# The last 52 rows of two Z blocks side by side in one buffer, contracted as two 64-row matmuls

## The chip, the cores and the metric

The kernel runs on one core of a Trainium2 chip. The core has a matrix engine (PE), a vector engine (DVE, VectorE), a scalar engine (ACT, ScalarE), GpSimd (POOL) and SP, which issues most of the transfers. Matmuls contract over the 128 partitions of on-chip memory (SBUF) and write to PSUM, eight banks of 512 fp32 values per partition. The metric is the device time of one execution in microseconds (us); 371.29 us is the median of the runs before.

## The reference

Two layers over x of 8 batches, 5696 positions and 128 channels: a long causal convolution by FFT, and a spectral mixing of its first 64 modes with a residual and a ReLU.

```python
L = 2 * S                                   # S = 5696
y = irfft(rfft(x, n=L, axis=1) * rfft(h, n=L, axis=0)[None], n=L, axis=1)[:, :S]

X = rfft(y, axis=1)
Y = zeros_like(X)
Xr, Xi = real(X[:, :64]), imag(X[:, :64])
Y[:, :64] = (einsum('bmd,mde->bme', Xr, w_r) - einsum('bmd,mde->bme', Xi, w_i)) + \
      1j * (einsum('bmd,mde->bme', Xr, w_i) + einsum('bmd,mde->bme', Xi, w_r))
u = y + irfft(Y, n=S, axis=1)
return u + maximum(u @ w_ch, 0)
```

## The kernel before, in words

The position is split as q*64 + p, with 89 values of q and J = 64 of p. The transforms are products with constant matrices, in fp16 with fp32 sums. The batches go in four groups of two (NP = 4).

In the first stage, for each group, PE transforms along q (`a_tile`, matmuls with F and Xin), then along p for each of 90 frequencies k (`second`, matmuls of 64 rows with As and M: batch 0 on partitions 0-63, batch 1 on 64-127, each to its own PSUM bank), the filter is multiplied in (`products`), a further product with W1 and W2 goes back along p (tile Zs or Zt), and the result is stored to a scratch array zs in HBM: 90 x 2 = 180 rows (real and imaginary part of each k) by 64 p by 256 values. Meanwhile `modes` sums up the 64 modes of the output spectrum (XT).

In the mode mixing, PE multiplies XT by the mode weights W, the result Y is transposed with an identity and becomes C, the coefficients of the second layer's inverse transform.

The last stage, the synthesis, makes u and the output. It reads zs back in blocks of ZB = 16 values of p: four blocks per group, 16 in all. A block has 180 rows: the first 128 go to a buffer ZTna (1024 KB), the other 52 to partitions 32 to 83 of a buffer ZTnb (416 KB), whose partitions 0 to 31 GpSimd has cleared once (`clear_zt`). There are NC = 5 such pairs of buffers. `u_tile(i, b, half)` makes eight values of p of block i for batch b, in two PSUM banks: for each bank one product of C with IBs (356 columns) and, for each of four values of p, one product of 89 columns with S4a (128 rows) and one with S4b (84 rows, 32 of them zeros). The tile is then read out to UT by ScalarE or VectorE (`n_ev` decides: VectorE takes counts 1, 4 and 6 of every 8; in the last group ScalarE takes all). The constants S4a and S4b are loaded by half and mirrored to the other half, S4a by VectorE and S4b by ScalarE (`reflect`).

`o_tile` multiplies four columns of 128 positions of UT by WI (w_ch beside an identity, 256 columns each); ScalarE writes the ReLU to R, VectorE adds and writes O, and SP stores to `out_dram`. Output tiles of one group stand between the synthesis tiles of the next; group 0 has none beside it. Both kinds of tile take PSUM banks in turn from four slots of two banks (`LSLOT`).

What sets the order: each engine runs its list in the order in which the program adds to it, and the recorder puts the waits in. SP's list holds the stores to zs, the constants, the block reads and the output stores, so a read waits for all that was added to SP before it. The dictionary `early` names the tick of the last group of stage one at which a read is added: S4b at 8, block 0 at 10, S4a at 12, identity and IBs at 14, block 1 at 16, block 3 at 19 and block 2 at 21; block 4 follows after the loop. From then on block i + 5 is added to SP's list when block i's tiles are done. Three tiles' S4 products are made ahead of need, among the mixing's products (`u_z(..., True)`, `ahead`); the first of them stands ahead of the mixing in PE's list.

All matmuls of this program are recorded at one line, 323, and all DMAs at line 320, so the tiles' names tell them apart.

Of the kernel before, what the change touches and what calls it, by code (L numbers as in the profile page):

```python
# [4 lines left out]
P = 128  # L5
# [118 lines left out]
def bass_long_conv_fft__then__afno_spectral_mix_kernel(nc, x, h, moe_w_r, moe_w_i, moe_w_ch, out):  # L124
# [40 lines left out]
    sg = np.ones((P, 3))  # L165
    sr = np.stack([(-1.0) ** kk, -(-1.0) ** kk], axis=1).reshape(2 * NK)
    sg[:, 0] = sr[0:P]
    sg[PB:PB + RB, 1] = sr[P:2 * NK]
    sg[M:P, 2] = -1.0
    tt = np.arange(S)  # L170
# [79 lines left out]
    wc_sb = at("Wc", 2 * P, F16, take(2 * P * 2))  # L250
    sg_sb = at("SG", 3, F32, take(12))
# [4 lines left out]
    ZB = 16  # L256
# [4 lines left out]
    zt_off = [(a_h, a_h2), (a_as1, a_as1 + 2 * ZP), (a_as1 + 4 * ZP, a_as1 + 6 * ZP), (a_h + 2 * ZP, a_h2 + 2 * ZP),  # L261
              (a_m2, a_g)]
    assert 2 * S + 8 * ZP <= AW * 2
    zt = [[at(f"ZT{i}{'ab'[p_]}", ZP, F16, zt_off[i][p_]) for p_ in range(2)] for i in range(NC)]
    ib_sb = at("IBs", S, F16, a_m)
    s4_sb = [at("S4a", S, F16, a_m + 2 * S), at("S4b", S, F16, a_as)]
    assert 4 * S + 2 * ZP + 4 * P + 2048 <= 2 * MW
# [31 lines left out]
    def bank(i):  # L299
        return ("bank", i)  # L300
# [226 lines left out]
    ZX = [("zs", i, b) for i in range(NZ, NZL) for b in range(2)]  # L527
    zt_old = [(H_ALL, H_ALL), (AST, AST), (AST, AST), (H_ALL, H_ALL), (M_ALL[3:6], G_ALL)]

    def load_zt(i):  # L530
        g_, c_ = divmod(i, J // ZB)
        for part, (p0, r0, n) in enumerate(((0, 0, P), (PB, P, RB))):
            old = list(once(("zt", i % NC, part), zt_old[i % NC][part]))
            dma("sync", bass.AP(zt[i % NC][part], p0 * ZP, [[ZP, n], [1, ZP]]),
                bass.AP(zs, (g_ * 2 * NK + r0) * J * 256 + c_ * ZB * 256, [[J * 256, n], [1, ZP]]),
                "t", [("zd", g_, s_) for s_ in range(NT)], [("zt", i % NC, part)], after=old)

    def clear_zt(i):
        z32 = zt[i][1][0:PB, :].bitcast(U32)
        R.add("gpsimd", lambda e: e.memset(z32, 0), (), [("zt0", i)], after=list(zt_old[i][1]) + pace)  # L540

    def load_ib():
# [11 lines left out]
    def load_s4(part):  # L554
        n = PB + RB if part else P
        dma("sync", s4_sb[part][0:n, 0:SH], bass.AP(c_s4, part * SH, [[2 * SH, n], [1, SH]]), "p", (),
            [("s4", part, 0)], after=AST if part else M_ALL[1:4])
# [13 lines left out]
    pace = []  # L571

# [176 lines left out]
    for g_ in range(NP):  # L749
        if g_ == NP - 1:  # L750
            load_w(0)
            load_w(1)
        for t in range(NT + LM):
            tick(g_, t)
            assert g_ + 1 < NP or not wp
            if g_ == NP - 1 and t in early:
                pace[:] = [("u", min(t, NT - 1) % NU)]
                early[t]()
        evac(bass.AP(xt, 2 * g_ + B, [[B * XTW, P], [B, 2], [3 * B, M], [1, 2]]), pv(MB, 0, [[M, 2], [1, M], [P, 2]]),
             [bank(MB)], [("xt", g_)], 1.0 / 64, eng="scalar", after=[("ag", k) for k in range(NS + 2 * XN, NK)])  # L760
        evac(bass.AP(xt, 2 * g_, [[B * XTW, P], [3 * B, M], [1, 2]]), pv(MB, M, [[1, M], [P, 2]]),
             [bank(MB)], [("xtn", g_)], -1.0 / 64, eng="vector" if g_ + 1 == NP else "scalar", after=[("ag", k) for k in range(NS + 2 * XN, NK)])
        if g_ + 1 < NP:
            for j in range(NB_, 32):
                a_tile(j, [(0, 4, 2, 6)[(j - 5) % 4]], "both" if j == 31 else (A, V)[(j - NB_) % 9 % 2])
                if j == 31:
                    second(g_ + 1, 0, 0, DA)
                if wp and j % 2 == 1:
                    dst, src_, ring, tok = wp.pop(0)
                    dma("gpsimd", dst, src_, ring, (), [tok], after=[("as", j)])  # L770


    pace[:] = []
    load_wi()
    for i in range(4, NC):
        load_zt(i)
        clear_zt(i)

# [4 lines left out]

    def u_z(i, b, half, alone=False, parts=(0, 1)):
        g_, c_ = divmod(i, NCH)
        t = ahead.get((i, b, half))
        if t is None:
            t = turns("l", LSLOT)
        z = zt[i % NC]
        for hb in parts:  # L790
            if not alone:
                u_c(i, b, half, t, hb, True)
            for pl in range(4):
                for ri in range(2):
                    pz = half * 8 + hb * 4 + pl
                    so = (c_ * ZB + pz) * NQ
                    n = (P, PB + RB)[ri]
                    mm(pv(t + hb, pl * NQ, [[1, NQ]]), z[ri][0:n, pz * 256 + b * P:pz * 256 + b * P + P], s4_sb[ri][0:n, so:so + NQ],
                       alone and pl == 0 and ri == 0, not alone and pl == 3 and ri == 1, [("zt", i % NC, ri), ("zt0", i % NC), ("s4", ri, 0)] + ([("s4", ri, 1)] if c_ >= NCH // 2 else []), [bank(t + hb)])
        if alone:  # L800
            ahead[(i, b, half)] = t
        return t

    def u_c(i, b, half, t, hb, first_):
        g_, c_ = divmod(i, NCH)
        pl0 = half * 8 + hb * 4
        mm(pv(t + hb, 0, [[1, 4 * NQ]]), c_sb[:, (2 * g_ + b) * P:(2 * g_ + b + 1) * P],
           ib_sb[:, (c_ * ZB + pl0) * NQ:(c_ * ZB + pl0 + 4) * NQ], first_, not first_,
           [("c", g_ // 2), ("ib", 0)] + ([("ib", 1)] if c_ >= NCH // 2 else []), [bank(t + hb)])

    def u_tile(i, b, half):
        g_, c_ = divmod(i, NCH)
        t = ahead.get((i, b, half))
        if t is None:
            t = u_z(i, b, half)
        else:
            for hb in range(2):
                u_c(i, b, half, t, hb, False)
# [5 lines left out]
        evac(bass.AP(u_sb[ub], c_ * ZB + half * 8, [[S, P], [J, NQ], [4, 2], [1, 4]]),  # L824
             src, [bank(t), bank(t + 1)], [("u_", ub, 2 * c_ + half)], eng=e, after=once(("u", ub), old))
# [32 lines left out]
    reflect("vector", ib_sb, P, 2, ("ib",), M_ALL[0:2])  # L858

# [52 lines left out]
    todo = []  # L912
    NB = NCH * NP
    NW4 = NW // 4
    for g_ in range(NP):
        last = g_ == NP - 1
        order = [(c_, b) for b in range(2) for c_ in range(NCH)] if last else [(c_, b) for c_ in range(NCH) for b in range(2)]
        for n, (c_, b) in enumerate(order):
            i = NCH * g_ + c_
            for half in range(2):  # L920
                u_tile(i, b, half)
                for _ in range((2, 2 + half)[n >= NCH] if last else 1 + half):
# [4 lines left out]
            if last and n == NCH - 1:  # L927
                todo += [(g_, 0, r4) for r4 in range(NW4)]
# [37 lines left out]
```

## Time and profile before

| | |
|---|---|
| median of 3 runs | 371.29 us (371.05 to 375.09) |
| profiled execution, first to last instruction | 370.1 us |
| PE busy, share of the span | 354.7 us, 96% |
| ACT busy | 316.2 us, 85% |
| DVE busy | 291.8 us, 79% |
| POOL busy | 75.2 us, 20% |
| DMA | 103.94 MB, mean 281 GB/s |

The profile gives of its own execution the span alone; the median lies 1.2 us above it. L323 is line 323 of the kernel. A row such as `ps<-S4b,ZT3b 84*128 84x89` is a matmul that writes PSUM from S4b and ZT3b, with 84 rows contracted, 128 columns of weights and 89 moving columns. `PEld` is the load of weights, which overlaps the matmuls. `SPq` is SP issuing a DMA: its duration is that of the issue, and the time to landing is told apart. In the timeline a row has its start, its duration (for merged rows, of all together), and in brackets the idle time of the engine before it with what ended it. Matmuls overlap: the step from one start to the next is what a matmul takes of PE.

### The profile page before, as it was taken

The numbers are of one execution on the slowest core, as the hardware profiler recorded it, in microseconds if no ns is written. First come the engines' busy times: TensorE is split into PE (matmuls) and PEld (weight loads), VectorE is DVE, ScalarE is ACT, GpSimd is POOL, SyncE is SP. The second block draws the span as 40 slices with busy tenths as digits, with TensorE's granted clock in tenths as the row PEclk, the third lists the DMA queues.
The fourth block names the chain that finished last, engine by engine and source line by source line (L and its number), as shares of the span: only waits on it lengthen the run. The fifth ranks groups of instructions, "written<-read, shape, count | busy, mean of one in ns | idle before, by whom it ended". The sixth has DMA issues, their size and how long they took to land.

```text
span 370.1 us, 12455 instructions
## 1 busy us (share of the span) xinstructions
PE 354.7 (96%) x5350; PEld 276.5 (75%) x5350; DVE 291.8 (79%) x332; ACT 316.2 (85%) x499; POOL 75.2 (20%) x117
## 2 busy tenths in 40 slices
PE   7999899999999999999999999999999999999994
PEld 7878766667866668866668766668899888888873
DVE  3549899988999999989999988775357777756666
ACT  8559999999999999999999999995467777688885
POOL 8804012100833311823213001151000000000000
PEclk9999999999999999999999999999999999999999
DMA  7999979969999996999996999999999999999878
GB/s 139 209 271 382 249 165 292 232 198 283 93 140 213 263 258 186 132 160 215 263 278 128 171 310 363 342 345 388 381 410 386 413 410 408 418 399 376 326 291 349
DMA packets 87048, 103.94 MB, mean 281 GB/s; under 512 B 22730, under 2 KB 72522, under 8 KB 83438
## 3 DMA queue, kind: packets, MB, share of 16 engines
q1 hardware_dynamic: 64610, 81.33, 62.5%
q0 software_dynamic: 22384, 21.83, 35.4%
q8 instruction: 42, 0.69, 0.7%
q14 instruction: 12, 0.10, 0.1%
HBM read 70.61 MB, written 51.12 MB: 329 GB/s over the span
## 4 chain that ended last, share of the span: by engine, by line
PE 78%; ACT 10%; DMA 7%; DVE 3%; issue 1%; POOL 1%; DVEq 0%; POOLq 0%
PE ps L323 78%; ACT As L313 6%; DMA out_dram<-O 5%; DMA Hin<-in_h_dram 2%; ACT R L898 1%; DVE As L317 1%; ACT Xs L311 1%; DVE U L623 1%; POOL Hin L320 1%; ACT UT L311 1%; DVE O L899 0%; ACT Zs L311 0%; DVE Hp L438 0%; ACT C L313 0%; DVE Hs L315 0%
## 5 line engine op out<-in xcount | busy, mean ns | idle before, releaser
L652 DVE TENSOR_TENSOR U<-Xs,Hs 128x2048 f16<-128x2048 f16 (+1 forms) x72 | 85.8, 1197 | 12.1 <-ACT Xs L311 11.5
L323 PE MATMUL ps<-U,Wc 128*128 128x512 f16 (+1 forms) x368 | 93.8, 376 | 1.4 <-DVE U L623 1.4
L311 ACT CAST Xs<-ps 128x1024 f16<-128x1024 f32 (+1 forms) x76 | 75.0, 995 | 5.8 <-PE ps L323 3.1
L311 ACT CAST Zs<-ps 128x512 f16<-128x512 f32 (+1 forms) x132 | 70.1, 605 | 0.7
L899 DVE TENSOR_TENSOR O<-ps,R 128x512 f32<-128x512 f32 x81 | 52.4, 684 | 21.6 <-ACT R L898 11.4
L898 ACT ACTIVATE R<-ps 128x512 f32<-128x512 f32 (+1 forms) x92 | 50.5, 592 | 8.5 <-PE ps L323 8.4
L317 DVE TENSOR_SCALAR As<-ps 128x720 f16<-128x720 f32 x64 | 53.1, 879 | 4.8 <-PE ps L323 3.3
L323 PE MATMUL ps<-As,M 64*128 64x128 f16 (+3 forms) x1504 | 52.5, 214 | 2.4 <-ACT As L313 1.2
L313 ACT ACTIVATE As<-ps 128x720 f16<-128x720 f32 (+1 forms) x68 | 48.2, 771 | 5.0 <-PE ps L323 4.8
L323 PE MATMUL ps<-F,Xin 128*128 128x180 f16 x512 | 52.1, 249 | 0.1
L323 PE MATMUL ps<-WI,UT 128*128 128x256 f16 x360 | 50.8, 278 | 0.5 <-ACT UT L311 0.4
L311 ACT CAST UT<-ps 128x712 f16<-128x712 f32 x46 | 34.5, 752 | 19.4 <-PE ps L323 18.4
L323 PEld LDWEIGHTS ps<-U,Wc 128*128 128x128 f16 x368 | 29.1, 97 | 28.2 <-DVE U L623 1.9
L323 PEld LDWEIGHTS ps<-F,Xin 128*128 128x128 f16 x512 | 45.2, 155 | 6.7 <-DVE Xin L365 0.9
L323 PEld LDWEIGHTS ps<-As,M 64*128 64x128 f16 x1504 | 42.2, 94 | 8.7 <-ACT Xs L311 1.9
L323 PEld LDWEIGHTS ps<-WI,UT 128*128 128x128 f16 x360 | 38.9, 152 | 3.2 <-issue 1.8
L323 PE MATMUL ps<-IBs,C 128*128 128x356 f16 x128 | 39.2, 314 | 0.8 <-DVE O L899 0.7
L320 POOL DMA_DIRECT2D Xt<-in_x_dram x40 | 21.4, 540 | 76.5 <-PE ps L323 76.0
L323 PEld LDWEIGHTS ps<-G,Zs 128*128 128x128 f16 x512 | 26.1, 96 | 14.1 <-ACT Zs L311 0.2
L652 DVE TENSOR_TENSOR U<-ps,Hs 128x2048 f16<-128x2048 f32 (+1 forms) x16 | 35.5, 2216 | 0.0
L323 PE MATMUL ps<-G,Zs 128*128 128x128 f16 (+2 forms) x512 | 31.9, 192 | 0.1
L311 ACT CAST Zt<-ps 128x512 f16<-128x512 f32 x52 | 29.1, 659 | 0.0
(76 smaller groups left out, 479.4 us busy)
## 6 DMA issues: line engine op xcount, KB each, us to landing
out_dram<-O SPq DMA_DIRECT2D x39, 512.0 KB, 10.5
zscr<-Zs SPq DMA_DIRECT2D x62, 256.0 KB, 6.7
zscr<-Zt SPq DMA_DIRECT2D x26, 256.0 KB, 6.6
Xt<-in_x_dram POOLq DMA_DIRECT2D x20, 320.0 KB, 6.9
W<-wscr SPq DMA_DIRECT2D x4, 1024.0 KB, 8.5
ZT0a<-zscr SPq DMA_DIRECT2D x4, 1024.0 KB, 11.0
M<-cM POOLq DMA_DIRECT2D x5, 720.0 KB, 17.6
ZT1a<-zscr SPq DMA_DIRECT2D x3, 1024.0 KB, 11.1
```

The costliest lines, as they stand in the source:

```text
L311: R.add(e, lambda h_: h_.copy(dst, src), reads, writes, after=after)
L313: R.add(e, lambda h_: h_.activation(dst, src, COPY, scale=scale), reads, writes, after=after)
L317: R.add(e, lambda h_: h_.tensor_scalar_mul(dst, src, scale), reads, writes, after=after)
L320: R.add(eng, lambda h_: h_.dma_start(dst, src), reads, writes, ring=ring, after=after)
L323: R.add("tensor", lambda h_: h_.matmul(o, l, r, start=st, stop=sp), reads, writes)
L623: R.add("vector", lambda e: e.tensor_tensor(bass.AP(u_s[0], b * 512 + d0, [[2048, P], [1024, 2], [D, n], [1, d1 - d0]]), bass.AP(s_[0], s_ ...
L652: R.add("vector", lambda e: e.tensor_tensor(uv, src, hv, MULT), bk + [("h", t, 0), ("h", t, 1, 0), ("h", t, 1, J)], [("u", i)])
L898: R.add("scalar", lambda e: e.activation(rv, src_r, RELU), bk, [("r", i % NR)], after=once(("r", i % NR), G_ALL + XTT + [("y", 0), ("y", 1 ...
L899: R.add("vector", lambda e: e.tensor_tensor(ov, src_u, rv, ADD), bk + [("r", i % NR)], [key + (h_,)], after=once(key, old))
```

## The change

Two blocks become a pair k (blocks 2k and 2k+1). The first 128 rows of each block keep a buffer of their own (`za`, seven of them). The other 52 rows of both blocks go into one buffer (`zb_`, three of them): those of block 2k to partitions 0-51, those of block 2k+1 to 64-115. Nothing is cleared any more. S4b holds the 52 rows twice likewise, each half with the columns of its own blocks; it is loaded whole (128 x 2848 values) and no longer mirrored.

A tile `u_tile(k, b, h4)` now takes four values of p from each block of the pair, one block per PSUM bank. Its order on PE is both products with IBs, eight with S4a (bank 0, then bank 1), then eight with S4b, of 52 rows, alternating between partitions 0-51 (bank 0) and 64-115 (bank 1). The number of matmuls is the same. The two reads of a pair's 52 rows are issued by SP for the first three pairs, and by ScalarE for pairs 3 to 7, when a pair's tiles are done; the next two `za` reads follow on SP.

```diff
-    RB, PB = 2 * NK - P, 32
+    RB, PB = 2 * NK - P, 64
...
-    s4t = np.zeros((P, 2 * SH))
-    s4t[:, 0:SH] = rows[0:P, 0:SH]
-    s4t[PB:PB + RB, SH:2 * SH] = rows[P:2 * NK, 0:SH]
+    s4b = np.zeros((P, S // 2))
+    for p0 in range(2):
+        s4b[p0 * PB:p0 * PB + RB] = rows[P:].reshape(RB, J // ZB // 2, 2, ZB * NQ)[:, :, p0].reshape(RB, S // 2)
+    s4t = np.concatenate([rows[0:P, 0:SH], s4b], axis=1)
...
-    NC = 5
+    NCA, NCB = 7, 3
...
+    def load_za(i):
         g_, c_ = divmod(i, J // ZB)
+        r_ = i % NCA
+        dma("sync", za[r_][:, :], bass.AP(zs, g_ * 2 * NK * J * 256 + c_ * ZP, [[J * 256, P], [1, ZP]]),
+            "t", zdone(g_), [("za", r_)], after=once(("za", r_), za_old[r_]))
+
+    def load_zb(k):
+        r_ = k % NCB
+        for p0 in range(2):
+            g_, c_ = divmod(2 * k + p0, J // ZB)
+            n = RB - RS
+            dma("scalar" if k >= NCB else "sync", bass.AP(zb_[r_], p0 * PB * ZP, [[ZP, n], [1, ZP]]),
+                bass.AP(zs, (g_ * 2 * NK + P) * J * 256 + c_ * ZP, [[J * 256, n], [1, ZP]]),
+                "t", zdone(g_), [("zb", r_, p0)], after=once(("zb", r_, p0), zb_old[r_]))
...
-             9: lambda: clear_zt(0),
-             10: lambda: load_zt(0),
+             10: lambda: (load_za(0), load_zb(0)),
              12: lambda: load_s4(0),
-             14: lambda: (load_id(), load_ib(), clear_zt(1)),
-             16: lambda: load_zt(1),
-             19: lambda: (load_zt(3), clear_zt(3)),
-             NT - 2: lambda: (load_zt(2), clear_zt(2))}
+             14: lambda: (load_id(), load_ib()),
+             16: lambda: load_za(1),
+             19: lambda: (load_za(2), load_zb(1)),
+             NT - 2: lambda: load_za(3)}
...
-    for i in range(4, NC):
-        load_zt(i)
-        clear_zt(i)
+    load_za(4)
+    load_zb(2)
+    load_za(5)
+    load_za(6)
...
+        for hb in range(2 if 0 in parts else 0):
+            z, r_ = za[(2 * k + hb) % NCA], (2 * k + hb) % NCA
             for pl in range(4):
+                pz = h4 * 4 + pl
+                so = ((c_ + hb) * ZB + pz) * NQ
+                mm(pv(t + hb, pl * NQ, [[1, NQ]]), z[:, pz * 256 + b * P:pz * 256 + b * P + P], s4_sb[0][:, so:so + NQ],
+                   alone and pl == 0, False, [("za", r_)] + ns, [bank(t + hb)])
+        r_ = k % NCB
+        for pl in range(4 if 1 in parts else 0):
+            pz = h4 * 4 + pl
+            so = (c_ // 2 * ZB + pz) * NQ
+            for hb in range(2):
+                r0 = hb * PB
+                mm(pv(t + hb, pl * NQ, [[1, NQ]]), zb_[r_][r0:r0 + RB, pz * 256 + b * P:pz * 256 + b * P + P],
+                   s4_sb[1][r0:r0 + RB, so:so + NQ], False, not alone and pl == 3,
+                   [("zb", r_, hb), ("s4", 1, 0)], [bank(t + hb)])
...
-    reflect("scalar", s4_sb[1], PB + RB, 1, ("s4", 1), AST)
...
-            if b == 1 and i + NC < NB:
-                load_zt(i + NC)
+            if b == 1:
+                if k + NCB < NPR * NP:
+                    load_zb(k + NCB)
+                for i in (2 * k, 2 * k + 1):
+                    if i + NCA < NCH * NP:
+                        load_za(i + NCA)
```

More of the change, by code (lines that the diff above doesn't have):

```diff
@@ L250, in bass_long_conv_fft__then__afno_spectral_mix_kernel @@
     wc_sb = at("Wc", 2 * P, F16, take(2 * P * 2))
-    sg_sb = at("SG", 3, F32, take(12))
+    sg_sb = at("SG", 2, F32, take(8))
     XTW = 3 * M
@@ L260, in bass_long_conv_fft__then__afno_spectral_mix_kernel @@
     a_as1, a_m2 = a_as + 2 * S, a_m + 4 * S
-    zt_off = [(a_h, a_h2), (a_as1, a_as1 + 2 * ZP), (a_as1 + 4 * ZP, a_as1 + 6 * ZP), (a_h + 2 * ZP, a_h2 + 2 * ZP),
-              (a_m2, a_g)]
+    za_off = [a_h, a_as1, a_h + 2 * ZP, a_as1 + 4 * ZP, a_as1 + 6 * ZP, a_m2, a_g]
+    zb_off = [a_h2, a_h2 + 2 * ZP, a_as1 + 2 * ZP]
     assert 2 * S + 8 * ZP <= AW * 2
-    zt = [[at(f"ZT{i}{'ab'[p_]}", ZP, F16, zt_off[i][p_]) for p_ in range(2)] for i in range(NC)]
+    za = [at(f"ZA{i}", ZP, F16, za_off[i]) for i in range(NCA)]
+    zb_ = [at(f"ZB{i}", ZP, F16, zb_off[i]) for i in range(NCB)]
     ib_sb = at("IBs", S, F16, a_m)
-    s4_sb = [at("S4a", S, F16, a_m + 2 * S), at("S4b", S, F16, a_as)]
+    s4_sb = [at("S4a", S, F16, a_m + 2 * S), at("S4b", S // 2, F16, a_as)]
     assert 4 * S + 2 * ZP + 4 * P + 2048 <= 2 * MW
@@ L527, in bass_long_conv_fft__then__afno_spectral_mix_kernel, with zdone @@
     ZX = [("zs", i, b) for i in range(NZ, NZL) for b in range(2)]
-    zt_old = [(H_ALL, H_ALL), (AST, AST), (AST, AST), (H_ALL, H_ALL), (M_ALL[3:6], G_ALL)]
-    def load_zt(i):
-        g_, c_ = divmod(i, J // ZB)
[L532 to L540, printed above, removed]
+    za_old = [H_ALL, AST, H_ALL, AST, AST, M_ALL[3:6], G_ALL]
+    zb_old = [H_ALL, H_ALL, AST]
+    def zdone(g_):
+        return [("zd", g_, s_) for s_ in range(NT)]
+    def load_za(i):
+        g_, c_ = divmod(i, J // ZB)
+        r_ = i % NCA
[9 more added lines that the diff above has]
+                "t", zdone(g_), [("zb", r_, p0)], after=once(("zb", r_, p0), zb_old[r_]))
     def load_ib():
@@ L782, in bass_long_conv_fft__then__afno_spectral_mix_kernel, with u_z @@
     ahead = {}
-    def u_z(i, b, half, alone=False, parts=(0, 1)):
-        g_, c_ = divmod(i, NCH)
-        t = ahead.get((i, b, half))
+    def u_z(k, b, h4, alone=False, parts=(0, 1)):
+        g_, c_ = divmod(2 * k, NCH)
+        t = ahead.get((k, b, h4))
         if t is None:
             t = turns("l", LSLOT)
[L789 to L792, printed above, removed]
-            for pl in range(4):
[L794 to L799, printed above, removed]
+        if not alone:
+            for hb in range(2):
+                u_c(k, b, h4, t, hb, True)
+        ns = [("s4", 0, 0)] + [("s4", 0, 1)] * (c_ >= NCH // 2)
+        for hb in range(2 if 0 in parts else 0):
+            z, r_ = za[(2 * k + hb) % NCA], (2 * k + hb) % NCA
+            for pl in range(4):
+                pz = h4 * 4 + pl
[6 more added lines that the diff above has]
+            so = (c_ // 2 * ZB + pz) * NQ
+            for hb in range(2):
+                r0 = hb * PB
+                mm(pv(t + hb, pl * NQ, [[1, NQ]]), zb_[r_][r0:r0 + RB, pz * 256 + b * P:pz * 256 + b * P + P],
+                   s4_sb[1][r0:r0 + RB, so:so + NQ], False, not alone and pl == 3,
+                   [("zb", r_, hb), ("s4", 1, 0)], [bank(t + hb)])
@@ L800, in u_z, with u_c @@
         if alone:
-            ahead[(i, b, half)] = t
+            ahead[(k, b, h4)] = t
         return t
-    def u_c(i, b, half, t, hb, first_):
-        g_, c_ = divmod(i, NCH)
-        pl0 = half * 8 + hb * 4
+    def u_c(k, b, h4, t, hb, first_):
+        g_, c_ = divmod(2 * k, NCH)
         mm(pv(t + hb, 0, [[1, 4 * NQ]]), c_sb[:, (2 * g_ + b) * P:(2 * g_ + b + 1) * P],
-           ib_sb[:, (c_ * ZB + pl0) * NQ:(c_ * ZB + pl0 + 4) * NQ], first_, not first_,
+           ib_sb[:, ((c_ + hb) * ZB + h4 * 4) * NQ:((c_ + hb) * ZB + h4 * 4 + 4) * NQ], first_, not first_,
@@ L823, in u_tile @@
         src = pv(t, 0, [[1, NQ], [512, 2], [NQ, 4]])
-        evac(bass.AP(u_sb[ub], c_ * ZB + half * 8, [[S, P], [J, NQ], [4, 2], [1, 4]]),
-             src, [bank(t), bank(t + 1)], [("u_", ub, 2 * c_ + half)], eng=e, after=once(("u", ub), old))
+        evac(bass.AP(u_sb[ub], c_ * ZB + h4 * 4, [[S, P], [J, NQ], [ZB, 2], [1, 4]]),
+             src, [bank(t), bank(t + 1)], [("u_", ub, 2 * c_ + h4)], eng=e, after=once(("u", ub), old))
     XTT = [(n, g_) for g_ in range(NP) for n in ("xt", "xtn")]
     reflect("vector", s4_sb[0], P, 0, ("s4", 0), M_ALL[1:4])
-    reflect("scalar", s4_sb[1], PB + RB, 1, ("s4", 1), AST)
     MC = 4
@@ L916, in bass_long_conv_fft__then__afno_spectral_mix_kernel @@
         last = g_ == NP - 1
-        order = [(c_, b) for b in range(2) for c_ in range(NCH)] if last else [(c_, b) for c_ in range(NCH) for b in range(2)]
+        order = [(c_, b) for b in range(2) for c_ in range(NPR)] if last else [(c_, b) for c_ in range(NPR) for b in range(2)]
         for n, (c_, b) in enumerate(order):
[L919 to L922, printed above, removed]
+            k = NPR * g_ + c_
+            for h4 in range(4):
+                u_tile(k, b, h4)
+                for _ in range((2, 2 + h4 % 2)[n >= NPR] if last else 1 + h4 % 2):
                     if todo:
                         o_tile(*todo.pop(0))
-            if b == 1 and i + NC < NB:
-                load_zt(i + NC)
-            if last and n == NCH - 1:
+            if b == 1:
[4 more added lines that the diff above has]
+                        load_za(i + NCA)
+            if last and n == NPR - 1:
                 todo += [(g_, 0, r4) for r4 in range(NW4)]
```

29 lines of the change are left out of this document (13 added, 16 removed).

## The prediction

> **What bounds the kernel now.** I read the page's busy line first, then busy time by stage, then single matmuls, then the transfers with their landing times. The last two of these windows are the synthesis that the change rewrites (it goes on to 357); 247.00:256.40 is the mode mixing before it, with the first products of that synthesis already in it.
>
> ```profile
> span 370.1 us, 12455 instructions
> PE 354.7 (96%) x5350; PEld 276.5 (75%) x5350; DVE 291.8 (79%) x332; ACT 316.2 (85%) x499; POOL 75.2 (20%) x117
> 247.00:256.40 9.40, 8.54 (x210) 7.71 (x208) 3.67 (x6) 5.80 (x8) 4.03 (x4) 1.00 1.07 373
> 256.40:270.40 14.00, 13.96 (x241) 11.99 (x242) 6.18 (x8) 6.67 (x9) 0.00 (x0) 1.00 1.01 390
> 270.40:317.00 46.60, 46.60 (x669) 41.99 (x666) 33.10 (x50) 33.92 (x58) 0.00 (x0) 1.00 1.01 405
> ```
>
> After the length of a stretch come PE, PEld, DVE, ACT and POOL, then the granted clock, the DMA share and GB/s. From 256.4 on PE has no hole, ACT works three quarters of the time at most until 317, and **the 16 DMA engines are full as well** (1.01). So two things set the end of this stage: what PE spends on a tile, and whether a block's read has landed when PE comes to it. How near the second is shows in the waits of PE's weight loads, in two rows of the timeline and in one piece of the chain that ended last:
>
> ```profile
> PEld ps L323 <- DMA ZT2b<-zscr: 0.3, 1, 0.3
> 336.13 0.21 PE L323 MATMUL ps<-S4b,ZT0b 84*128 84x89 f16 x1 [0.16 <-DMA ZT0b<-zscr]
> 338.32 0.31 PE L323 MATMUL ps<-IBs,C 128*128 128x356 f16 x1 [0.33 <-DVE O L899]
> 320.68 16.68 DMA out_dram<-O
> ```
>
> PE already waits for a read twice, and once for DVE, which was held by an output store that took 16.68 us to land and free its buffer. The idle time in brackets counts from the end of the matmul before, and in a stream the next one starts some 0.16 before that end (duration 0.20, step 0.04, rows below); so the steps lost are about 0.3, 0.3 and 0.5 us.
>
> **What a tile costs.** One synthesis tile is, per PSUM bank, one product with IBs and eight of 89 columns. Rows of one bank, then a place where 64-row matmuls (As,M) stand between 128-row ones, and one with 64 columns:
>
> ```profile
> 300.10 0.31 PE L323 MATMUL ps<-IBs,C 128*128 128x356 f16 x1
> 300.25 0.20 PE L323 MATMUL ps<-S4a,ZT3a 128*128 128x89 f16 x1
> 300.29 0.21 PE L323 MATMUL ps<-S4b,ZT3b 84*128 84x89 f16 x1
> 300.59 0.32 PE L323 MATMUL ps<-IBs,C 128*128 128x356 f16 x1
> 301.08 0.30 PE L323 MATMUL ps<-WI,UT 128*128 128x256 f16 x1
> 130.05 0.27 PE L323 MATMUL ps<-G,Zs 128*128 128x128 f16 x2
> 130.10 0.22 PE L323 MATMUL ps<-G,Zs 128*128 128x128 f16 x1
> 130.25 1.07 PE L323 MATMUL ps<-As,M 64*128 64x128 f16 x32
> 131.10 0.22 PE L323 MATMUL ps<-As,M 64*128 64x128 f16 x2
> 131.25 0.39 PE L323 MATMUL ps<-U,Wc 128*128 128x512 f16 x1
> 31.95 0.41 PE L323 MATMUL ps<-Ah,M 64*128 64x64 f16 x16
> 32.29 0.30 PE L323 MATMUL ps<-F,Xin 128*128 128x180 f16 x1
> ```
>
> Look at start times, not durations. Eight 89-column products take 0.34 us (300.25 to 300.59), 0.0425 each, and a tile 0.98 us (300.10 to 301.08). The 32 As products are 16 pairs, one on partitions 0-63 and one on 64-127, each to its own bank: 15 steps from 130.25 to 131.10 are 0.057 per **pair**, what one 128-column product takes alone (130.05 to 130.10). So pairs do run side by side. But the step from the last G product to the first As is 0.15 instead of 0.055, and out again 131.10 to 131.25 is 0.15: **a change between 128 and 64 rows costs PE 0.095 us, each way.** For 64 columns, 0.34 less one such exit leaves 0.031 a pair; a line between 64 and 128 columns gives 0.041 for a pair of 89.
>
> **The change, part by part.**
>
> *Side-by-side products.* A tile's eight S4b products (0.34) become four pairs (4 x 0.041 = 0.164) and two changes of rows (0.19): 0.354, so +0.014; if a pair steps like today's single product, 0.0425, +0.02; with 0.01 more for the first pair, +0.03. Order matters here: the new code puts all S4a products first, so it is two changes per tile, not sixteen. I take +0.02: 64 tiles make +1.3 us, the 48 of pairs 2 to 7 +1.0 (0.7 to 1.4). **What is halved is given back by the switching.** [...]
>
> *What must have landed when.* The reads and their landings:
>
> ```profile
> S4b<-cS SPq DMA_DIRECT2D x1, 481.9 KB
> 241.31 0.56 SPq L320 DMA_DIRECT2D ZT1a<-zscr  x1
> ZT1a<-zscr SPq DMA_DIRECT2D x1, 1024.0 KB, 7.7
> 257.67 2.29 SPq L320 DMA_DIRECT2D ZT4a<-zscr  x1
> ZT4a<-zscr SPq DMA_DIRECT2D x1, 1024.0 KB, 10.2
> 261.25 1.31 SPq L320 DMA_DIRECT2D ZT0a<-zscr  x1
> ZT0a<-zscr SPq DMA_DIRECT2D x1, 1024.0 KB, 10.3
> ZT4b<-zscr SPq DMA_DIRECT2D x1, 416.0 KB
> 248.85 0.20 PE L323 MATMUL ps<-S4a,ZT0a 128*128 128x89 f16 x1
> 249.94 0.25 PE L323 MATMUL ps<-XT,W 128*128 128x64 f16 x3 [0.21 <-issue]
> 270.46 0.20 PE L323 MATMUL ps<-S4a,ZT4a 128*128 128x89 f16 x1
> 277.16 0.20 PE L323 MATMUL ps<-S4a,ZT0a 128*128 128x89 f16 x1
> ```
>
> SP's queue is a line: between ZT4a's landing (267.9) and that of block 5 in ZT0a (271.55) it moved 416 + 1024 KB in 3.7 us, 389 KB/us. So 416 KB are 1.07 us, 1024 KB 2.6. Today the first products, at 248.85, need block 0 alone. A tile of the new code takes half of its columns from each block of a pair, so they need block 1 (za1) too. Today its rows land at 241.31 + 7.7 = 249.0. Ahead of them stand now a second 52-row read (1.07) and an S4b of 128 x 2848 values, 712 KB for 482 (0.6): 250.7. PE, in order, then makes four products, two changes and four pairs, about 0.6, and mixing starts at 251.3 for 249.94: **1.4 us late**, with nothing to hide it.
>
> The next such place is worse. Pair 2 starts where block 4 does (270.46), but its second bank needs block 5 within 0.3 us, at 270.8 on today's clock, where today block 5 is wanted at 277.16. PE gets there 1.4 + 16 x 0.02 - 0.3 = 1.4 us late, at 272.2. Block 5's 128 rows (za5) land at 271.55 + 0.6 + 1.07 (one more 52-row read ahead) = 273.2 if they have the DMA engines to themselves. They have not: after pair 0 (PE at about 264) ScalarE issues zb3, 832 KB, on its own queue. Two queues at work at once:
>
> ```profile
> zscr<-Zs SPq DMA_DIRECT2D x1, 256.0 KB, 9.9
> WI<-in_moe_w_ch_dram POOLq DMA_DIRECT2D x1, 32.0 KB, 8.4
> ```
>
> Both were issued between 248.2 and 248.7; GpSimd's small read landed in the midst of SP's line, not behind it. If ScalarE's read gets equal turns, its 832 KB (2.1 us) are all moved before za5's last row: 275.3. So PE stands 2.4 us (alone) to 4.5 us (shared) late at pair 2; the 1.4 is inside that, since one wait swallows the other. I take 4.5, the row with two queues being the nearest. [...]
>
> Later pairs have their reads long before: za7 and zb3 are issued a whole pair ahead of pair 3, which starts some 13 us on.
>
> *ScalarE's issuing.* Ten issues, two after each of pairs 0 to 4. They wait for PE's last product of the pair, which ScalarE's own read of that tile has waited for already, so the wait is nothing. The issue itself, and what lies about it:
>
> ```profile
> 262.60 1.40 SPq L320 DMA_DIRECT2D ZT0b<-zscr  x1
> 285.93 0.46 SPq L320 DMA_DIRECT2D ZT0b<-zscr  x1
> ```
>
> Queued behind it is the next R. That needs a whole tile (0.98, read out by VectorE at this place in the turn) and an output tile (four matmuls, about 0.44) of PE first: 1.4 us for two issues of 0.46. I cost it at 0; at 1.40 each, ScalarE is 1.4 us late after each of four pairs.
>
> *Removed for nothing:*
>
> ```profile
> 249.47 2.60 ACT L550 ACTIVATE S4b<-S4b,SG 84x2759 f16<-84x2759 f16 x1
> 252.30 0.59 ACT L311 CAST Y<-ps 128x512 f16<-128x512 f32 x1 [0.24 <-PE ps L323]
> 249.19 1.83 POOL L540 MEMSET ZT4b<- 32x2048 uint32 x1
> ```
>
> ScalarE mirrors S4b in 2.6 us, then still waits 0.24 for PE; the five memsets lie on GpSimd, for which no PE wait stands in the list. Both are worth 0. Output tiles, evacuations (same element counts) and the tail stay.
>
> *Sum.* +4.5 at pair 2, +1.0 for switching in pairs 2 to 7, and -0.8 for the two later waits on DMA, which a later PE no longer meets: **+4.7 us**. The profiled execution has a span of 370.1; the median of the runs, 371.29, lies 1.2 above it, which I carry over: **376.0 us**.
>
> **Rivals.**
>
> *ScalarE's reads don't hold za5 up* (the engines serve the older queue first, or zb3 starts late). For it: the POOL read still took 8.4 us, hardly less than SP's. Against: it was 64 KB in all, in many small rows. 2.4 + 1.0 - 0.8 = +2.6: **373.9**.
>
> *The changes of rows are hidden, and it is not slower.* If a change costs little between 89-column products, a tile saves up to 0.176; 48 of them are 8.4 against 4.5 - 0.8. From 0.05 us a change downward the stage no longer loses; at zero, 3.9 us are gained with the waits on stores still there: **368**. Against it: in the As rows both ways cost the same 0.095, beside 128 columns and beside 512. [...]
>
> *ScalarE is blocked by its issues*, 1.40 each as at 262.60, PE 0.7 to 1.4 late in each of four pairs: +3 to 5.6 more, about **380**. SP's long issues come with a full line, which ScalarE's queue is not.
>
> *It doesn't do what it says:* 52 rows don't run as pairs. Then 0.34 + 0.19 for 0.34, +0.19 a tile, 9.1 in the last 48 on 4.5 - 0.8: **384**.
>
> **How the numbers follow.** Forecast 0.46 (374.9 to 377.5); first rival 0.28; hidden switching 0.09; blocked ScalarE 0.11; no pairs 0.04; the rest in between. About 1% (3.7 us) is what a measurement of this kernel can tell from no change: slower is over 375.0, and takes nearly all of the forecast, blocked and unpaired; same takes the first rival and half of the hidden one. The range leaves out hidden switching below and the unpaired case with the far half of the blocked one above: 372.3 to 379.5.
>
> **What would show it.** First S4a product near 248.9 but the second bank's, on za1, near 250.7; mixing from 251.3; pair 2's second bank waiting on za5 until 273 (first rival) or 275 (forecast); two S4b products starting nearly together every 0.041, with steps of about 0.14 before and after; a tile of 1.0 us; ScalarE's issues below 0.5. The prediction is wrong if za1 or za5 land before PE comes, if 52-row products start without the 0.095, or if PE's later holes (stores, reads) grow instead of going.

## The result, and the profile after

The changed kernel takes **391.93 us** in the median of four runs (388.81 to 393.80); the kernel before took 371.38 beside it (371.05 to 375.09). The ratio is **1.052, with a 95% interval of 1.048 to 1.057**: 5% slower. The prediction was 376.0 with a range of 372.3 to 379.5. The direction came out, the size did not: +20 us instead of +4.7.

The page of before first, with the shares of the chain that ended last; then the page of the changed kernel, with span, busy times and the same shares; then its windows, which are those shown of before with 270.4 to 317 cut in two and one stretch added. After the length of a stretch come PE, PEld, DVE, ACT, POOL, the granted clock, the DMA share and GB/s:

```profile
PE 78%; ACT 10%; DMA 7%; DVE 3%; issue 1%; POOL 1%; DVEq 0%; POOLq 0%
```

```profile
span 389.6 us, 12443 instructions
PE 362.0 (93%) x5350; PEld 273.7 (70%) x5350; DVE 291.8 (75%) x332; ACT 314.0 (81%) x498; POOL 66.1 (17%) x112
PE 62%; DMA 18%; ACT 11%; DVE 4%; issue 2%; SPq 1%; POOL 1%; DVEq 0%; POOLq 0%; ACTq 0%
```

```profile
247.00:256.40 9.40, 6.18 (x89) 4.49 (x87) 2.75 (x4) 3.29 (x8) 0.00 (x0) 0.81 1.08 371
256.40:270.40 14.00, 13.30 (x253) 10.88 (x251) 4.57 (x6) 4.95 (x7) 0.00 (x0) 0.88 1.05 332
270.40:300.00 29.60, 22.63 (x314) 17.59 (x313) 11.46 (x16) 12.38 (x20) 0.00 (x0) 0.83 0.99 300
300.00:317.00 17.00, 17.00 (x239) 14.12 (x238) 12.45 (x19) 11.99 (x21) 0.00 (x0) 1.00 0.99 378
317.00:335.00 18.00, 16.15 (x201) 13.06 (x200) 10.43 (x15) 10.81 (x20) 0.00 (x0) 0.91 1.02 383
```

The busy times hardly differ, and the chain now runs through transfers for 18% of the span, 70 us, for 7%, 26 us, before. In the windows, look at the last two columns together. From 270.4 to 300 the DMA engines are as busy as before (0.99), but they move **300 GB/s where they moved 405**. The change adds next to nothing to move: S4b's 230 KB in the whole kernel, and those earlier. Here a full DMA share says that the engines are occupied, not that they deliver.

PE shows where this lands. These are its three longest waits between 245 and 330 (in total, times, longest), then one of VectorE between 315 and 330, and rows of PE's timeline:

```profile
PE ps L325 <- DMA ZA<-zscr: 8.7, 2, 7.0
PE ps L325 <- DVE O L911: 1.9, 1, 1.9
PE ps L325 <- ACT Zs L313: 1.3, 1, 1.3
DVE O L911 <- DMA out_dram<-O: 2.2, 1, 2.2
```

```profile
253.79 0.33 PE L325 MATMUL ps<-S4a,ZA 128*128 128x89 f16 x2 [1.76 <-DMA ZA<-zscr]
...
268.34 0.48 PE L325 MATMUL ps<-IBs,C 128*128 128x356 f16 x2
268.65 0.50 PE L325 MATMUL ps<-S4a,ZA 128*128 128x89 f16 x8
269.08 0.34 PE L325 MATMUL ps<-S4b,ZB 52*128 52x89 f16 x8
269.36 0.33 PE L325 MATMUL ps<-IBs,C 128*128 128x356 f16 x1
...
285.10 0.26 PE L325 MATMUL ps<-S4a,ZA 128*128 128x89 f16 x1 [6.97 <-DMA ZA<-zscr]
...
324.31 0.31 PE L325 MATMUL ps<-IBs,C 128*128 128x356 f16 x1 [1.85 <-DVE O L911]
```

The two waits for za1 and za5 stand where the prediction put them, but the second ends at 285.10 instead of 275.3. A third hole, at 324.31, is a wait for VectorE, which itself waited 2.2 us for an output store. Milestones against before: first C product 256.41 before and 263.25 after; start of block 4 and of pair 2 270.31 and 277.48; last C product 356.65 and 375.81. So 7 us are lost before pair 2, 7 at za5, and 5 later. One tile, from 268.34 to 269.36, takes 1.02 us.

### The profile page after: what moved, and what is told of

It is laid out like the page before. It is cut to its first block, busy times and chain, and to the rows that moved or that the text cites. A ratio compares the mean times of both kernels' runs of the same rounds, so it can differ in the third digit from the quotient of the medians.

```text
span 389.6 us, 12443 instructions
## 1 busy us (share of the span) xinstructions
PE 362.0 (93%) x5350; PEld 273.7 (70%) x5350; DVE 291.8 (75%) x332; ACT 314.0 (81%) x498; POOL 66.1 (17%) x112
## 4 chain that ended last, share of the span: by engine, by line
PE 62%; DMA 18%; ACT 11%; DVE 4%; issue 2%; SPq 1%; POOL 1%; DVEq 0%; POOLq 0%; ACTq 0%
PE ps L325 62%; DMA ZA<-zscr 7%; ACT As L315 6%; DMA out_dram<-O 5%; DMA Hin<-in_h_dram 2%; DMA Xt<-in_x_dram 2%; DMA zscr<-Zs 2%; ACT Xs L313 2%; SPq L322 1%; DVE As L319 1%; ACT Zs L313 1%; ACT R L910 1%; DVE U L629 1%; POOL Hin L322 1%; ACT UT L313 1%
## 5 line engine op out<-in xcount | busy, mean ns | idle before, releaser
L911 DVE TENSOR_TENSOR O<-ps,R 128x512 f32<-128x512 f32 x81 | 52.7, 687 | 25.3 <-ACT R L910 14.5
L325 PE MATMUL ps<-WI,UT 128*128 128x256 f16 x360 | 54.1, 290 | 0.6 <-ACT UT L313 0.3
L313 ACT CAST UT<-ps 128x712 f16<-128x712 f32 x46 | 34.8, 756 | 17.9 <-PE ps L325 17.6
L325 PEld LDWEIGHTS ps<-WI,UT 128*128 128x128 f16 x360 | 39.7, 152 | 7.1 <-issue 1.3
L325 PE MATMUL ps<-S4a,ZA 128*128 128x89 f16 x512 | 33.4, 208 | 8.7 <-DMA ZA<-zscr 8.7
L325 PEld LDWEIGHTS ps<-S4a,ZA 128*128 128x128 f16 x512 | 29.5, 101 | 15.9 <-DMA ZA<-zscr 9.0
L325 PE MATMUL ps<-IBs,C 128*128 128x356 f16 x128 | 30.1, 321 | 2.1 <-DVE O L911 1.9
```

What stands on the lines that cost most here:

```text
L313: R.add(e, lambda h_: h_.copy(dst, src), reads, writes, after=after)
L325: R.add("tensor", lambda h_: h_.matmul(o, l, r, start=st, stop=sp), reads, writes)
L911: R.add("vector", lambda e: e.tensor_tensor(ov, src_u, rv, ADD), bk + [("r", i % NR)], [key + (h_,)], after=once(key, old))
```

## The experiments

Two theories stood at first. **Place:** a 52-row read that lands within one half of the 128 partitions (0-51 or 64-115) moves more slowly than one on 32-83, which reaches into both halves. **Queue:** the reads that ScalarE issues on a second queue delay SP's.

### Reads alone

A kernel of reads only (of x, in rows of 8 KB), of the sizes that matter here (1024 KB on 128 rows, 416 KB on 52 rows), in nine phases, each begun when the last has landed. It was executed once; its output is zeros.

```diff
+    phase([(SY, 0, P, i) for i in range(8)])
+    phase([(SY, 32, 52, i) for i in range(12)])
+    phase([(SY, 0, 52, i) for i in range(12)])
+    phase([(SY, 64 * (i % 2), 52, i) for i in range(12)])
+    phase([((SY, AC)[i % 2], 64 * (i % 2), 52, i) for i in range(12)])
+    phase([q for i in range(6) for q in ((SY, 0, P, i), (AC, 32, 52, 6 + i))])
+    phase([q for i in range(6) for q in ((SY, 0, P, i), (AC, 64 * (i % 2), 52, 6 + i))])
+    phase([q for i in range(6) for q in ((SY, 0, P, i), (SY, 32, 52, 6 + i))])
+    phase([q for i in range(6) for q in ((SY, 0, P, i), (SY, 64 * (i % 2), 52, 6 + i))])
```

> Left out: the whole computation; the output is zeros. Only reads of 8 KB rows of x into SBUF, in nine phases, each begun when the one before has landed: (1) 8 reads of 128 rows on SP; (2) 12 of 52 rows to partitions 32-83 on SP; (3) 12 to 0-51 on SP; (4) 12 alternately to 0-51 and 64-115 on SP; (5) the same, SP and ScalarE in turn; (6) 6 of 128 rows on SP beside 6 of 32-83 on ScalarE; (7) the same with 0-51 and 64-115 on ScalarE; (8) as 6, all on SP; (9) as 7, all on SP. Theory 'place' (a 52-row read that lands within one half of the 128 partitions moves at half the speed): 8 x 2.5 = 20 us, then 12 x 1.2 = 15, then 24 to 30 for phases 3 and 4, phase 5 between 15 and 30, phases 6 and 8 about 22, phases 7 and 9 30 or more. Theory 'queue' (ScalarE's own queue beside SP's is what slows the reads): phases 2, 3 and 4 alike at 15, phases 6 and 7 alike and longer than 8 and 9, which are 22.

The windows of this kernel, one row per phase in the order of the code (PE and ACT have no work in them and no column):

```profile
0.73:23.09 22.36, 0.91 (x1) 0.00 (x0) 1.00 0.92 375
23.09:40.26 17.17, 0.00 (x0) 0.00 (x0) 1.00 0.73 298
40.26:72.20 31.94, 0.00 (x0) 0.00 (x0) 1.00 0.75 160
72.20:101.95 29.75, 0.00 (x0) 0.00 (x0) 1.00 0.75 172
101.95:124.48 22.53, 0.00 (x0) 0.00 (x0) 1.00 0.72 227
124.48:148.69 24.21, 0.00 (x0) 0.00 (x0) 1.00 0.89 366
148.69:180.85 32.16, 0.00 (x0) 0.00 (x0) 1.00 0.90 275
180.85:205.45 24.60, 0.00 (x0) 0.00 (x0) 1.00 0.87 360
205.45:239.77 34.32, 0.00 (x0) 0.00 (x0) 1.00 0.84 258
```

Twelve 52-row reads take 17.17 us on 32-83 and **31.94 on 0-51** (1.43 and 2.66 us a read), at nearly the same DMA share (0.73 and 0.75) and with the same bytes. Turning between the halves on one queue helps little (29.75); one queue for each half helps (22.53). Beside 128-row reads, as in the kernel, the place is worth 9.72 us in six reads on SP alone (34.32 less 24.60), **1.62 us a read**. The second queue, in the same place, costs nothing (24.21 against 24.60). For the rate of the reads, place holds and queue falls; which read lands first on two queues is another matter, and comes up below.

The rates by place: 160 and 172 GB/s with one half at a time, 227 with a queue for each half, 298 on 32-83, 375 on all 128 rows. What makes the difference was not shown.

### Before, with its 52 rows moved to 64-115

```diff
-    RB, PB = 2 * NK - P, 32
+    RB, PB = 2 * NK - P, 64
```

> The kernel before with one number changed: the 52 rows land on partitions 64-115 instead of 32-83 (PB = 64), with zeros in 0-63; still one 128-row matmul each, on SP, same order of reads. S4b grows from 84 to 116 rows (0.5 us of transfer). Theory 'place': each of the 16 reads takes up to 1.2 us more of queues that are full; the stores and reads behind them come later, so 8 to 16 us slower (379 to 387). Theories 'queue' and 'need' (a tile that draws on two blocks needs the second one earlier): nothing of theirs is in this kernel, within 1 us of before.

One number changes, no pairs, no ScalarE's reads, the same order; with the place S4b grows from 84 to 116 rows. It takes **399.38 us** (397.67 to 401.44), ratio 1.071 (1.065 to 1.078). This is far beyond the 379 to 387 that the place theory expected. Worked out afterwards from the reads alone, 16 reads at 1.62 us are 26 us; measured are 26.5 over the 372.9 of before beside it. Its window over the stretch where before moved 405 GB/s, then some of its waits:

```profile
270.40:317.00 46.60, 41.46 (x578) 36.52 (x579) 23.91 (x34) 25.07 (x42) 0.00 (x0) 0.93 1.01 298
```

```profile
ACT Zs L311 <- DMA zscr<-Zs: 4.7, 3, 2.4
DVE O L899 <- DMA out_dram<-O: 10.6, 4, 4.2
PE ps L323 <- DVE O L899: 9.6, 6, 3.3
```

The lost transfer time reaches PE mostly through stores. Some 7 us are lost before the first tile (first C product at 263.55, before at 256.41), where ScalarE waits for stores of Zs. Later the largest waits are for output stores (VectorE 10.6 us for them, PE 9.6 for VectorE): a store that lands late keeps VectorE from its next sum, and that keeps the output tile's PSUM banks. So the place alone is enough to cost as much as the whole change did, whatever the tiles look like.

### Before, with the new order of tiles

The reads, their places and the 84-row products of before; only the tile takes four values of p from each block of a pair, and two reads are added after each pair. It has five buffers as before.

```diff
-            for pl in range(4):
+            i = 2 * k + hb
...
-                    pz = half * 8 + hb * 4 + pl
+                    pz = h4 * 4 + pl
...
-            if b == 1 and i + NC < NB:
-                load_zt(i + NC)
+            if b == 1:
+                for i in (2 * k, 2 * k + 1):
+                    if i + NC < NB:
+                        load_zt(i + NC)
```

> The kernel before with its five pairs of buffers, its reads on partitions 32-83, SP alone and 84-row matmuls, but each tile takes four values of p from each of two neighbouring blocks, as in the changed kernel, and blocks 2k+5 and 2k+6 are read when pair k is done. Theory 'need': PE waits for block 1 at about 250 and for block 5 at about 272, 1.4 to 3 us each, and its clock halves after such a hole; +4 to +9 us (375 to 380). Theory 'place': only what a fast read leaves, +2 to +4. If both holes are there as in the changed kernel (7 us at block 5), 'place' falls.

It takes **380.95 us** (380.54 to 381.41), ratio 1.022 (1.015 to 1.028). Its waits on reads:

```profile
250.93 0.21 PE L323 MATMUL ps<-S4b,ZT1b 84*128 84x89 f16 x1 [0.76 <-DMA ZT1b<-zscr]
...
273.42 0.21 PE L323 MATMUL ps<-S4b,ZT0b 84*128 84x89 f16 x1 [0.97 <-DMA ZT0b<-zscr]
...
339.27 0.26 PE L323 MATMUL ps<-S4a,ZT0a 128*128 128x89 f16 x1 [4.47 <-DMA ZT0a<-zscr]
```

Blocks 1 and 5 are waited for, as the prediction said, but for 0.76 and 0.97 us only. The hole at 339.27 is this kernel's own: with five buffers block 15 can be asked for only when pair 5 is done. The 8 us that it loses in all are therefore beyond what theory 'place' expected, and the number alone would suit 'need'. But by the starts of the 64 casts that read the tiles out to UT, against those of before, it is 2.4 us late from pair 2 to the end of the third group, and the rest comes with the hole at 339.27. So the need for both blocks of a pair costs about 2.4 us by itself; it does not make 7 us at block 5.

### The changed kernel with all reads on SP

```diff
-            dma("scalar" if k >= NCB else "sync", bass.AP(zb_[r_], p0 * PB * ZP, [[ZP, n], [1, ZP]]),
+            dma("sync", bass.AP(zb_[r_], p0 * PB * ZP, [[ZP, n], [1, ZP]]),
```

> The changed kernel with all reads of the 52 rows issued by SP. Theory 'queue': block 5's rows land near 275 instead of 285, the hole of 7 us at pair 2 goes down to 1 to 3, 5 us or more are gained (387 or less). Theory 'place': the reads still land in one half of the partitions, and block 5 gains only what pair 3's read took in front of it (2 to 4 us); total 386 to 391.

It takes 387.26 us (386.57 to 392.36), ratio 1.041 (1.033 to 1.050), an interval that touches that of the changed kernel; the median is 4.7 us lower. The profiled execution is the longest of the four, 392.36; the other three took 386.57, 387.01 and 387.52. Two rows of its timeline:

```profile
280.37 0.21 PE L325 MATMUL ps<-S4a,ZA 128*128 128x89 f16 x1 [1.56 <-DMA ZA<-zscr]
...
305.22 0.46 PE L325 MATMUL ps<-IBs,C 128*128 128x356 f16 x1 [4.46 <-DVE O L911]
```

za5 now comes 4.7 us earlier (280.37 against 285.10) and its hole is 1.56 us for 6.97, so ScalarE's reads did hold it up, as theory 'queue' had it. In this execution the time comes back at 305.22, as a wait for VectorE, which waited 5.4 us for an output store. Whether that hole stood in the three shorter executions is not known, as they have no trace. So neither theory falls here: **some 5 of the 20 us may be the second queue's** (4.7 by the medians, 6.2 when each is taken against the runs of before beside it), and some 14 over before stay with all reads on SP.

### The changed kernel with half of the 52 rows

Each read brings 26 of the 52 rows, to partitions 32-57 and 96-121, and zeros stand in 0-31 and 64-95. Half of the rows are not read, and those that are stand against other rows of S4b, so the result is not that of the kernel; every product and its size stay.

```diff
-            n = RB - RS
-            dma("scalar" if k >= NCB else "sync", bass.AP(zb_[r_], p0 * PB * ZP, [[ZP, n], [1, ZP]]),
+            n = RB // 2
+            dma("scalar" if k >= NCB else "sync", bass.AP(zb_[r_], (p0 * PB + 32) * ZP, [[ZP, n], [1, ZP]]),
...
+    def clear_zb(r_):
+        for p0 in (0, PB):
+            z32 = zb_[r_][p0:p0 + 32, :].bitcast(U32)
```

> The changed kernel, but each read of 52 rows brings only 26 of them (left out: half of the last 52 rows' contribution; zeros stand in partitions 0-31 and 64-95, the 26 rows land on 32-57 and 96-121; the matmuls keep 52 rows). By m1 a 52-row read to one half takes about 2.6 us and to 32-83 1.3; 26 rows to one half should take as long as 52 rows spread. Theory 'place': this gives back the whole of what the place costs and leaves what the prediction counted (need, switching): 374 to 380. Rivals: if the order of need and the second queue make the holes, it stays above 385.

Reckoned from the reads alone (half of 2.66 us is 1.33, for 1.43), half of the rows in one half of the partitions take about as long as all of them on 32-83; no phase has 26 rows. So this is nearly the kernel that the prediction reckoned with. It takes **378.88 us** (378.41 to 379.86), ratio 1.016 (1.013 to 1.020), 13.0 less than the changed kernel. Its timeline, with the first products of the synthesis, the beginning of the mixing and pair 2, and two windows:

```profile
249.65 0.49 PE L325 MATMUL ps<-S4a,ZA 128*128 128x89 f16 x8
...
250.74 1.03 PE L325 MATMUL ps<-XT,W 128*128 128x64 f16 x30 [0.32 <-issue]
...
271.77 0.33 PE L325 MATMUL ps<-S4a,ZA 128*128 128x89 f16 x4
275.62 0.48 PE L325 MATMUL ps<-S4a,ZA 128*128 128x89 f16 x4 [3.52 <-DMA ZA<-zscr]
```

```profile
275.62:281.20 5.58, 5.58 (x44) 4.04 (x45) 1.92 (x3) 2.13 (x4) 0.00 (x0) 0.50 1.02 285
281.20:290.00 8.80, 8.80 (x127) 7.38 (x126) 6.54 (x10) 6.08 (x11) 0.00 (x0) 1.00 0.98 410
```

PE reaches the second bank of pair 2 at 272.1 (predicted 272.2) and gets za5 at 275.62 (predicted 275.3); mixing begins at 250.74 (251.3). After the hole the clock is 0.50 for the whole of the first window. In 5.58 us PE does the work of 2.8 at the full clock (5.58 x 0.50); the prediction had no such term. A limit of this run: it also moves half of the bytes, so 13.0 us (14.4 when each is taken against the runs of before beside it) is the place and whatever the missing bytes are worth in the rest of the stage.

The starts of the casts to UT, one for each tile, tell how late a kernel is against before. In us, in the profiled executions, with the last C product on PE as the last column:

| | last tile ahead of pair 2 | first tile of pair 2 | two tiles on | last tile of the third group | last C product |
|---|---|---|---|---|---|
| half of the rows | 1.1 | 5.1 | 7.3 | 8.4 | 6.7 |
| as changed | 7.1 | 14.5 | 16.6 | 21.0 | 19.2 |

So what goes with half of the rows goes in three places: 6.0 us before pair 2, 3.4 at za5, and 3.3 where the changed kernel has its hole at 324.31.

### The changed kernel with the hole filled

Is the half clock after the hole a cause of its own in the changed kernel? Forty-four products that nobody reads, 6.6 us, stand in PE's list ahead of pair 2, so that PE is not idle:

```diff
+        if (k, b, h4) == (2, 0, 0):
+            for _ in range(44):
+                mm(pv(t, 0, [[1, 4 * NQ]]), c_sb[:, 0:P], ib_sb[:, 0:4 * NQ], True, True, [("c", 0), ("ib", 0)], [bank(t)])
```

> The changed kernel with 44 products of 356 columns (0.15 us each, 6.6 us in all, results overwritten) put into PE's list ahead of pair 2's first tile, where PE otherwise idles for 7 us waiting for block 5. Theory 'clock' (a hole of some us halves the granted clock for the work after it): the clock stays at 1.00 through 275 to 295, about 2.7 us gained. Without it: the same time, or up to 1 us slower where the hole is shorter than the filling.

One of its windows, and PE's two longest waits from 265 on:

```profile
270.40:300.00 29.60, 27.74 (x371) 21.23 (x369) 11.74 (x16) 12.71 (x21) 0.00 (x0) 1.00 0.99 306
```

```profile
PE ps L325 <- DVE O L914: 3.1, 2, 1.7
PE ps L325 <- DMA ZA<-zscr: 1.9, 1, 1.9
```

The clock stays at 1.00 where it was 0.83, and the time is **392.21 us** (391.14 to 392.76), ratio 1.051 (1.048 to 1.055), the same as without. The 2.7 us that theory 'clock' expected are not seen. The traces give two reasons: in this execution za5 comes 1.85 us later than in that of the changed kernel (286.95 for 285.10), for which the filling gives no cause, and PE waits 1.0 us more for VectorE (3.1 for 2.1).

```profile
286.95 0.26 PE L325 MATMUL ps<-S4a,ZA 128*128 128x89 f16 x2 [1.86 <-DMA ZA<-zscr]
```

That the transfers set the time here whatever the clock does (306 GB/s at a share of 0.99) fits this, but is argued, not shown. The half clock about the mode mixing was not tried.

### Before, with a second queue

```diff
-            dma("sync", bass.AP(zt[i % NC][part], p0 * ZP, [[ZP, n], [1, ZP]]),
+            dma("scalar" if part and i >= NC else "sync", bass.AP(zt[i % NC][part], p0 * ZP, [[ZP, n], [1, ZP]]),
```

> The kernel before, with the 52-row reads of blocks 5 to 15 issued by ScalarE, landing on 32-83 as ever. Theory 'place' (with m1: two queues cost nothing): within 1% of before, perhaps 0.5 us faster, as PE's waits on these reads shorten. Theory 'queue', or a ScalarE held up by issuing: 2 us or more slower.

372.90 us (371.23 to 376.21, ten runs), ratio **1.001 (0.997 to 1.004)**. ScalarE's issues and a second queue cost this kernel nothing, as the prediction had it for ScalarE's part.

### The changed kernel with a queue for each half

The reads alone took 22.5 us with one queue for each half and 31.9 with one half at a time, so the changed kernel might gain from it: SP reads partitions 0-51, ScalarE 64-115, from pair 3 on.

```diff
-            dma("scalar" if k >= NCB else "sync", bass.AP(zb_[r_], p0 * PB * ZP, [[ZP, n], [1, ZP]]),
+            dma("scalar" if k >= NCB and p0 else "sync", bass.AP(zb_[r_], p0 * PB * ZP, [[ZP, n], [1, ZP]]),
```

> The changed kernel, but from pair 3 on SP issues the read for partitions 0-51 and ScalarE that for 64-115, so that the two halves are filled at once. By m1 12 reads in turns took 29.7 us from one queue and 22.5 from two. Theory 'place': 10 reads gain up to 0.6 us each, 2 to 6 us faster than the changed kernel. Theory 'queue': no gain, since two queues still share the engines.

A miss for theory 'place': 395.40 us (393.78 to 398.23), ratio 1.059 (1.054 to 1.064), no gain, as 'queue' expected, and the wait at za5 is still 6.50 us. A likely reason is that SP's line is deep (its 128-row reads land 17.9 us after their issue in the median) and ScalarE's empty, so that the two halves of a pair were not filled at the same time; this is argued, not shown.

No kernel here beats the one before.

## Why the prediction was wrong, step by step

**The step that failed** is "So 416 KB are 1.07 us". That is the rate of SP's line over 416 KB on partitions 32 to 83 and 1024 KB on all 128, put on reads that land on 0-51 and 64-115. The size is the same, the place is not. In the reads alone a 52-row read takes 2.66 us in one half and 1.43 on 32-83; beside 128-row reads one half costs 1.33 us more on two queues (32.16 less 24.21, by six) and 1.62 more on one. Sixteen of them are 21 to 26 us of transfer time in a stage whose DMA engines were already full. The prediction quoted that fullness (1.01 and 405 GB/s) and asked only when single reads would land; it never asked what the whole stage would need if a read became dearer. The changed kernel lost 20, of which 13.0 go with half of the rows. That the direction came out is no merit of the sum: its largest term stands at the right place with a wrong price, and none of the four rivals has the place of the rows in it.

**What is left without the place.** With the place taken out (half of the rows) 13.0 us go, and 378.88 stays against the 376.0 that the prediction summed up; against before it is +6.2 (372.7 beside it) for a forecast of +4.7.

**First products on za1.** With half of the rows mixing begins at 250.74 for 251.3, but that is luck: PE doesn't wait for za1 there at all. It comes to the first products 0.8 us late (249.65 for 248.85), for a reason that stays open, and makes both banks without a break; the prediction itself named a za1 that has landed before PE comes as a sign of its being wrong. In the changed kernel the wait is there, but mixing begins at 254.62, 4.7 us late for 1.4. There, by the waits of ScalarE between 245 and 260,

```profile
ACT Zs L313 <- DMA zscr<-Zs: 1.6, 1, 1.6
```

it waited 1.6 us for a store of Zs to land, and PE 1.3 us for ScalarE. The first S4a product was late by 2.9 us (251.71, before 248.85), and PE then waited 1.76 us more for za1. Both are transfers in a stretch whose DMA share is 1.08 (247.00 to 256.40); that the slower 52-row reads held them up is argued, not shown.

**Pair 2 on za5.** Right in place. The forecast was 4.5 us from 270.8; it was 14 (285.10). The sharing with ScalarE's zb3 is real: 4.7 us between all on SP and as changed, for 2.1 in the prediction; at half the speed zb3's 832 KB would be 4.3. What it is worth in the whole time is open: in the traced execution with all on SP the time came back at an output store, but the median is 4.7 us lower. The first rival, by which ScalarE's reads don't hold za5 up, falls.

**Side-by-side products.** Pairs run side by side: the eight 52-row products and the change back take 0.28 us (269.08 to 269.36), less than the 0.34 of eight single ones. A change of rows costs 0.093 to 0.097 us in the trace after, as read from the As rows. So the rivals with a hidden change and with no pairs fall (the first of them adds up to 367.4, 371.3 less 3.9, not 368). A tile takes 1.02 us for 0.98, +0.035 to 0.04 where +0.02 was taken and 0.03 the upper bound. Over 48 tiles that is 1.7 to 1.9 us for 1.0. What is halved is indeed given back by the switching.

**ScalarE's issuing at 0.** Right in its cost, though two pairs of the ten issues (median 0.40 us) took 0.6 and 0.97 us each in the mean, not below 0.5. These two pairs in the timeline of the changed kernel (for two issues together) are

```profile
269.47 1.21 ACTq L322 DMA_DIRECT2D ZB<-zscr  x2
277.60 1.94 ACTq L322 DMA_DIRECT2D ZB<-zscr  x2
```

The second fell into the hole at za5, where nothing waited for ScalarE; its longer issue, 1.60 us, had at most three reads ahead of it on ScalarE's queue, where the prediction had laid SP's long issues to a full line. Before with a second queue takes the same time as before. The rival with a blocked ScalarE falls.

**−0.8 for later waits.** (By its row, one of the two is a wait for VectorE behind a store.) With half of the rows it came: no PE wait over 0.3 us is left from 300 to 360. In the changed kernel it did not, and the hole at 324.31 (1.85) took its place, as the prediction named among the signs of its being wrong.

**A term that was missing altogether** is the clock after a hole: 2.8 us of work with half of the rows. In the changed kernel the mixing at half clock (0.51 from 252.80 to 259.70) takes 2.2 us longer up to the first C product (254.62 to 263.25, for 249.94 to 256.41), and two tiles after za5 another 2.1 are lost; whether the whole time feels them is open. With this term the case of half rows adds up to 4.8 (za5) + 2.8 + 1.7 - 0.8 = 8.5 against 6.7 measured at the last C product (363.34, the second of a pair of rows that begins at 363.19, for 356.65). By the table above, za5 and the clock make 7.3 and the switching 1.1 up to the end of the third group, near enough to the terms. In the last group the sum lets 0.2 come back (0.8 less 0.6 of switching) and 1.7 do; why, stays open.

## What to carry to other kernels

When an edit moves the destination of a transfer, price the transfer anew: 52 rows inside one half of the partitions moved at about half the speed of 52 rows across the middle (160 for 298 GB/s), though bytes, row size and queue were the same. Here the 64-row products put each operand into one half, so the cost of filling them belongs beside what PE gains. And where the DMA share is 1.0 as well as PE's, look at GB/s and sum up the stage's transfer time; waiting times of single reads only tell where the loss will show.

## What the runs showed of the hardware that was not expected

Place: 160 GB/s on 0-51 against 298 on 32-83 for the same reads, and 227 with both halves filled from two queues. So the place in the kernel before, whose 84-row products carry 32 zero rows, pays for itself: with one number changed to move it, that kernel loses 26.5 us.

The granted clock. These are windows of the changed kernel, cut where it stood at 0.5 (by windows of 0.7 us, to about that much):

```profile
252.80:259.70 6.90, 5.91 (x106) 5.49 (x107) 0.74 (x1) 0.59 (x1) 0.00 (x0) 0.51 1.09 350
280.10:290.40 10.30, 5.30 (x43) 3.93 (x44) 1.64 (x3) 1.95 (x3) 0.00 (x0) 0.50 1.02 278
324.50:327.90 3.40, 3.40 (x28) 2.50 (x27) 2.10 (x4) 0.69 (x2) 0.00 (x0) 0.50 1.04 421
```

They last 6.9, 10.3 and 3.4 us. A hole of 1.85 us was enough to bring one on (324.31), and within the long hole the clock fell some 2 us after PE had stopped (at 278.13, the 285.10 of its row less 6.97). But with the hole filled, one of 1.86 us (286.95) left the clock at 1.00, so the length of a hole alone doesn't decide; what does was not shown. What PE lost by it behind za5 was 2.1 us over two tiles in the changed kernel and 2.8 us of work with half of the rows.
